# A gated delta-rule layer with a gated MLP: the first two groups' inverses made from two halves, and work moved between slots

## The chip, the core and the metric

The kernel runs on one core of a Trainium2 chip. Its engines are TensorE (PE in the profile), VectorE (DVE), ScalarE (ACT), GpSimd (POOL) and SyncE (SP), which here issues all DMAs. Each engine works through its own instructions in order and waits for others by semaphores. The metric is the device time of one execution in microseconds; the time before is 690.91 us, the median of 3 runs (690.77 to 692.4).

## The reference

```python
def _attn_ref(q, k, v, beta):                     # q, k, v: (4, 8, 768, 48)
    k_n = k / (np.linalg.norm(k, axis=-1, keepdims=True) + 1e-06)
    state = np.zeros((B, H, D, D))
    for t in range(S):
        kt, vt, bt = (k_n[:, :, t], v[:, :, t], beta[:, :, t, None])
        y[:, :, t] = np.einsum('bhd,bhde->bhe', q[:, :, t], state)
        v_old = np.einsum('bhde,bhd->bhe', state, kt)
        state = state + bt[:, :, :, None] * np.einsum('bhd,bhe->bhde', kt, vt - v_old)

def _moe_ref(x, w_gate, w_val, w_out):            # x: (3072, 384), d_ff = 1536
    gate = 1.0 / (1.0 + np.exp(-(x @ w_gate)))
    return (gate * (x @ w_val)) @ w_out
```

The first part is a recurrence over 768 tokens for 32 heads; its rows, put together over the heads, go through the gated MLP.

## The kernel before

**Groups.** The 768 tokens are cut into 12 groups of 64. A group is 64 tokens of all 32 heads (256 rows of x). Within a group the recurrence is solved in closed form: for each head the Gram matrix of its 64 keys is made (`gram`, L228), the norms of the keys are taken from its diagonal (`norms`, L182), and a triangular system of 32 rows is inverted on DVE for all heads at once (`solve`, L265): 31 columns from the last to the first, two DVE instructions each (L283, L286), over a tile X of 128 x 16 x 32, then a 32x32 block transposition into `mt` (L288). Two blocks of 32 tokens make up the 64: `updates` (L313) multiplies `mt` with the right-hand side of the first block (step 0), subtracts the coupling through L (step 1), and multiplies `mt` with the second block (step 2). The results U go from PSUM (`pu`) to SBUF (`su`) by four copies. `masked` (L247) makes the products of queries and keys (`pp`), which four DVE instructions mask (L260); `rows` (L339) makes the outputs from U, the masked products and the state; `advance` moves the state on; `flip` transposes the rows into x and splits them into a high and a low part for TensorE's float32r (`xx`).

**MLP.** For each group, 12 tiles f of 128 hidden units: `gate_val` (18 matmuls, `gv`), sigmoid on ACT, product on DVE (`gated`), a split into high and low parts (`split_hi` on ACT, `split_lo` on DVE, tile `h`), and `outp` (6 matmuls into `po`, which runs over all 12 tiles). `outp` runs LAG = 2 tiles behind `gate_val`.

**Weights.** They arrive as 36 pieces of 128 x 384 eight-byte words and are turned into two float32r parts by five instructions: two on ACT (`scaled`), a join on DVE (`u`), the high part on ACT (`weight_hi`), the low part on DVE (`weight_lo`). Before slot 0 the first 14 pieces are scaled; the other steps are spread over slots 0 to 20.

**Order.** The order of every engine's instructions is written out by hand. First comes a prologue for group 0 (L478 to L520). Then the program runs in slots: an MLP tile is two slots, `gate_val` at the start of the even one, `outp` at the start of the odd one; behind these come the functions that `plan[s]` lists, then the splits and the gating. Group g's attention runs in the slots of group g-1's MLP, which begin at slot w = 24(g-1). PSUM has four pools of two banks: `seq`, `aux`, `gv`, `po`. The two banks of `aux` hold in turn the Gram products, the masked products, `pu`, the rows and the flipped x, so each of these waits until the one before has been read.

Of the kernel before, what the change touches and what calls it, by code (L numbers as in the profile page):

```python
# [55 lines left out]
def deltanet_gated_mlp(ctx: ExitStack, tc: tile.TileContext, kd, qd, kv, beta, words, out):  # L56
# [20 lines left out]
    zero = const.tile([128, 1], F32, name="zero")  # L77
    xx = [const.tile([128, 2, KC, GT], F32R, name=f"xx{i}") for i in range(2)]

# [26 lines left out]
    def constants():  # L106
# [52 lines left out]
    def join(n):  # L159
        half, lo, hi = words_of(n)  # L160
        us[n] = u = wk.tile([128, PW], U32, name=f"u_{n}", tag="u", bufs=4)
        nc.vector.scalar_tensor_tensor(out=u, in0=hi, scalar=3, in1=lo, op0=ALU.logical_shift_left, op1=ALU.bitwise_or)  # L162
# [11 lines left out]
    def converting():  # L174
        for n in range(len(pieces) + 2):
            for m, fn in ((n, join), (n - 1, weight_hi), (n - 2, weight_lo)):
                if 0 <= m < len(pieces):
                    fn(m)
                yield

# [47 lines left out]
    def gram(g):  # L228
# [9 lines left out]
        for e in range(2):  # L238
            js = slice(e * J, (e + 1) * J)

            for lo, hi, o in ((0, 128, 0), (32, 64, 32), (96, 128, 32)):
                nc.scalar.copy(G[lo:hi, :, js], pg[e][lo:hi, :, o:o + 32].rearrange("q p t -> q t p"))  # L242
            for t in (0, 64):
                lo, o = t + 32 * e, 32 - 32 * e
                nc.scalar.copy(L[lo:lo + 32, js], pg[e][lo:lo + 32, :, o:o + 32])

# [18 lines left out]
    def solve(g):  # L265
# [47 lines left out]
    def updates(g, step):  # L313
# [5 lines left out]
        if step == 1:  # L319
# [6 lines left out]
            return  # L326
        pu = ps_aux.tile([128, J, D], F32, name=f"pu_{g}_{step}", tag="aux")
        for j in range(J):
            for e, x in KINDS:
                r = at[e, x][step // 2]  # L330
                nc.tensor.matmul(out=pu[r:r + 32, j], lhsT=mt[r:r + 32, e * J + j], rhs=R[e][r:r + 32, j], start=True, stop=True)  # L331
        for e, x in KINDS:
            r = at[e, x][step // 2]
            if g == 0 and x:
                nc.vector.tensor_copy(out=su[r:r + 32, 3 if x else e], in_=pu[r:r + 32])
            else:
                nc.scalar.copy(su[r:r + 32, 3 if x else e], pu[r:r + 32])  # L337

# [48 lines left out]
    def flip(g, c):  # L387

        st = state[g]
        if c == 0:  # L390
            st["xh"], st["xl"] = (xx[g % 2][:, i] for i in range(2))
# [25 lines left out]
    def split_hi(g, f):  # L417
        st = state[g]
        st["hh", f] = hh = wk.tile([128, 2, GT], F32R, name=f"h_{g}_{f}", tag="h", bufs=3)
        nc.scalar.copy(hh[:, 0], st["sg", f])  # L420
# [25 lines left out]
    W = 2 * NF  # L446
    LAG = 2
    plan = collections.defaultdict(list)
# [22 lines left out]

    NORMS, SOLVE = 18, 66
    conv = converting()


# [14 lines left out]
    stage(14, len(pieces))  # L490
    constants()
    gram(0)
# [16 lines left out]
    updates(0, 1)  # L509
    take(conv, 3)  # L510
    take(masks0, 2)
    updates(0, 2)
    take(masks0, 2)
    rows(0)
    take(conv, 3)
    load_k(2)
    load_q(2)
    flip(0, 0)
    flip(0, 1)
    take(conv, 3)  # L520
    ahead = 14
    pre1 = chain(norms(1), solve(1))
    spread(conv, 3 * (len(pieces) - 3), 0, W - 3)
    for n in range(ahead, len(pieces)):
        plan[(n - ahead) * 2 // 3].append(lambda n=n: scaled(n))
    spread(pre1, NORMS + SOLVE, 0, 12)
    plan[4].append(lambda: scale_v(1))
# [10 lines left out]
    for g in range(N):  # L538
# [89 lines left out]
```

## Time and profile before

| | |
|---|---|
| median of 3 runs | 690.91 us |
| profiled execution | 693.46 us, span 691.8 us, granted TensorE clock 0.967 |
| PE busy | 619.6 us (90%) |
| DVE busy | 490.7 us (71%) |
| ACT busy | 321.6 us (46%) |
| first gate_val of group 0 | 53.5 us |
| first gate_val of group 1 | 147.7 us |
| from one group to the next, later | 49.8 us |

How to read the rows: a row of the timeline is start, duration, engine, source line, operation, output tile <- input tiles, partitions x elements, and a count where equal instructions were merged; in brackets stands how long the engine had been idle and what ended that. "The chain of waits" is the chain of work that ended last, followed back from the end. The table of stretches gives, for each stretch of the span, the busy time of each engine, the granted clock of TensorE (1.00 is full speed), and DMA.

### The profile page before, as it was taken

To read this page: it belongs to the slowest core of one execution; us is meant where nothing else is said; L and a number is where in the kernel's file an instruction comes from. 1 tells how busy PE (TensorE), PEld (TensorE's weight loads), DVE (VectorE), ACT (ScalarE), POOL (GpSimd) and SP (SyncE) were. 2 spreads that over 40 slices of the span, in tenths; PEclk is the share of its full clock that TensorE was granted. 3 is DMA by queue.
4 is the path that set the end of the run, shared out by engine and by line. 5 is a ranking of instruction groups with operands and counts; after the bars stand their busy time and mean duration, and the time that the engine had idled before them with its cause. 6 is when DMAs were issued, how large, how long until landed. Compare 5 with 4: busy or idle time off the path is not lost.

```text
span 691.8 us, 22994 instructions
## 1 busy us (share of the span) xinstructions
PE 619.6 (90%) x9992; PEld 592.2 (86%) x9992; DVE 490.7 (71%) x1533; ACT 321.6 (46%) x877; POOL 7.4 (1%) x21
## 2 busy tenths in 40 slices
PE   3166755889999999999999999999999999999997
PEld 3155745889899999999999999999999999999996
DVE  4859498997796696687778778768768867852321
ACT  6827665734534634643543542543544445333322
POOL 4000000000000000000000000000000000000000
PEclk9999677989999999999999999999999999999999
DMA  9995000021021111211210211210210210010101
GB/s 262 338 400 123 21 5 1 2 78 47 4 79 47 24 57 48 57 42 31 79 25 26 79 25 26 79 36 15 79 48 3 79 26 3 1 25 4 24 1 23
DMA packets 17765, 41.00 MB, mean 59 GB/s; under 512 B 4224, under 2 KB 7296, under 8 KB 17664
## 3 DMA queue, kind: packets, MB, share of 16 engines
q1 hardware_dynamic: 17664, 39.53, 19.7%
q8 instruction: 78, 1.28, 0.8%
q14 instruction: 23, 0.19, 0.1%
HBM read 34.80 MB, written 4.72 MB: 57 GB/s over the span
## 4 chain that ended last, share of the span: by engine, by line
PE 70%; DVE 18%; DMA 5%; issue 3%; ACT 3%; SPq 1%; ACTq 0%; DVEq 0%
PE gv L409 37%; PE po L435 19%; DVE kqp L260 3%; PE pu L331 3%; DMA kv<-in_kv_dram 3%; DVE X L286 2%; DVE tmp L283 2%; DMA raw<-in_words_dram 2%; PE yy L360 2%; PE yy L357 2%; PE pg L237 2%; PE pk L300 2%; DVE gp L187 2%; DVE w L172 2%; DVE u L162 1%
## 5 line engine op out<-in xcount | busy, mean ns | idle before, releaser
L409 PE MATMUL gv<-xx,w 128*128 128x256 f32 x2592 | 350.9, 291 | 7.9 <-DVE w L172 5.5
L409 PEld LDWEIGHTS gv<-xx,w 128*128 128x128 f32 x2592 | 337.8, 197 | 12.3 <-DVE w L172 6.6
L435 PE MATMUL po<-w,h 128*128 128x384 f32 x864 | 183.6, 349 | 6.2 <-DVE h L425 6.2
L435 PEld LDWEIGHTS po<-w,h 128*128 128x128 f32 x864 | 146.5, 192 | 11.2 <-DVE h L425 7.9
L420 ACT CAST h<-sg 128x256 fp32r<-128x256 f32 x144 | 58.4, 405 | 178.4 <-DVE sg L415 178.0
L415 DVE TENSOR_TENSOR sg<-sg,gv 128x256 f32<-128x256 f32 x144 | 60.2, 418 | 71.9 <-ACT sg L414 70.8
L283 DVE TENSOR_TENSOR tmp<-X,gp 128x126 f32<-128x126 f32 (+22 forms) x372 | 94.6, 254 | 10.9
L286 DVE TENSOR_TENSOR X<-X,tmp 128x126 f32<-128x126 f32 (+22 forms) x372 | 94.7, 254 | 10.2
L425 DVE TENSOR_TENSOR h<-sg,h 128x256 fp32r<-128x256 f32 x144 | 60.5, 420 | 56.4 <-ACT h L420 56.1
L414 ACT ACTIVATE sg<-gv 128x256 f32<-128x256 f32 x144 | 55.2, 383 | 80.9 <-PE gv L409 80.1
L337 ACT COPY su<-pu 32x384 f32<-32x384 f32 x92 | 43.2, 470 | 23.0 <-PE pu L331 21.5
L226 ACT ACTIVATE kv<-kv,mq 128x48 f32<-128x48 f32 x192 | 44.5, 323 | 0.2 <-DVE mq L220 0.2
L242 ACT COPY G<-pg 32x256 f32<-32x256 f32 (+1 forms) x72 | 26.4, 367 | 20.0 <-PE pg L237 18.6
L237 PE MATMUL pg<-kqp 48*64 48x64 f32 x768 | 17.8, 245 | 19.7 <-DMA kqp<-in_kd_dram 10.0
L237 PEld LDWEIGHTS pg<-kqp 48*64 48x64 f32 x768 | 15.5, 156 | 22.7 <-issue 15.6
L260 DVE TENSOR_TENSOR kqp<-pp,pmask 64x512 f32<-64x512 f32 x48 | 32.9, 686 | 1.1
L331 PE MATMUL pu<-R,mt 32*32 32x48 f32 x1408 | 20.3, 206 | 11.5 <-DVE kqp L260 6.4
L331 PEld LDWEIGHTS pu<-R,mt 32*32 32x32 f32 x1408 | 17.4, 107 | 15.2 <-PE gv L409 6.6
L311 DVE TENSOR_TENSOR R<-kv,pk 128x384 f32<-128x384 f32 x44 | 22.3, 549 | 11.2 <-PE pk L300 9.9
L167 ACT CAST w<-u 128x384 fp32r<-128x384 f32 x36 | 18.2, 510 | 18.6 <-DVE u L162 18.4
L397 ACT CAST xx<-pt 128x384 fp32r<-128x384 f32 x24 | 11.5, 480 | 29.4 <-PE pt L395 29.3
L172 DVE TENSOR_TENSOR w<-u,w 128x384 fp32r<-128x384 f32 x36 | 19.7, 551 | 5.8 <-ACT w L167 5.7
(65 smaller groups left out, 417.5 us busy)
## 6 DMA issues: line engine op xcount, KB each, us to landing
raw<-in_words_dram SPq DMA_DIRECT2D x36, 384.0 KB, 7.8
kv<-in_kv_dram SPq DMA_DIRECT2D x24, 384.0 KB, 4.1
kqp<-in_qd_dram SPq DMA_DIRECT2D x24, 256.0 KB, 3.9
kqp<-in_kd_dram SPq DMA_DIRECT2D x24, 192.0 KB, 3.5
out_dram<-ot SPq DMA_DIRECT2D x48, 96.0 KB, 2.2
beta<-in_beta_dram SPq DMA_DIRECT2D x12, 16.0 KB, 3.8
```

What stands on the lines that cost most here:

```text
L226: nc.scalar.activation(V[:, c], V[:, c], AF.Copy, scale=mq[:, c, 0:1])
L237: nc.tensor.matmul(out=pg[e][t:t + 64, j], lhsT=kq[r:r + D, x, j], rhs=kq[r:r + D, x, j], start=True, stop=True)
L260: nc.vector.tensor_tensor(out=kq[t:t + 64, sec], in0=pp[e][t:t + 64], in1=pmask[t:t + 64, e].unsqueeze(1).to_broadcast([64, J, C]), op=ALU ...
L283: nc.vector.tensor_tensor(out=tmp, in0=X[:, k:16, j:j + 1].to_broadcast([128, n, j]), in1=gp[:, j:j + 1, 0:j].to_broadcast([128, n, j]), o ...
L286: nc.vector.tensor_tensor(out=X[:, k:16, 0:j], in0=X[:, k:16, 0:j], in1=tmp, op=ALU.add)
L331: nc.tensor.matmul(out=pu[r:r + 32, j], lhsT=mt[r:r + 32, e * J + j], rhs=R[e][r:r + 32, j], start=True, stop=True)
L409: nc.tensor.matmul(out=pg[:, o], lhsT=parts[w, f][:, a, k * 128:(k + 1) * 128], rhs=x[b][:, k], start=(k == 0 and q == 0), stop=(k == KC - ...
L414: nc.scalar.activation(h, st["gv", f][:, 0], AF.Sigmoid)
L415: nc.vector.tensor_tensor(out=h, in0=h, in1=st["gv", f][:, 1], op=ALU.mult)
L420: nc.scalar.copy(hh[:, 0], st["sg", f])
L425: nc.vector.tensor_tensor(out=hh[:, 1], in0=st["sg", f], in1=hh[:, 0].bitcast(F32), op=ALU.subtract)
L435: nc.tensor.matmul(out=po[s], lhsT=hh[:, a, ts], rhs=parts["o", f][:, w], start=(f == 0 and q == 0), stop=(f == NF - 1 and q == 2))
```

## The change

1. Groups 0 and 1 are solved by `solve_halves`: the two diagonal 16x16 blocks of each 32x32 system are inverted side by side (15 columns, two instructions each, on a tile of 128 x 2 x 8 x 16), put into X and transposed, and the lower left block is joined on TensorE by two sets of 64 matmuls of 32x32 (`pz`, `pm`), with a copy on ACT, a transposition and a subtraction on DVE. The lower left block is taken from G by `lower_left` (ACT, with a mask `under` as scale). Groups 2 to 11 keep `solve`.
2. In the prologue: G is copied ahead of L for both halves; group 1's Gram product comes behind group 0's solve instead of ahead of it; group 0's masks come ahead of and behind the first U; U of the two kinds goes through two PSUM banks, one copied by ACT and one by DVE; conversion has another order, and 8 pieces are scaled ahead instead of 14.
3. In the slots: the Gram product of group 2 moves from slot 3 to 14, its masked product from 6 to 22; the solve of group 2 starts in slot 16 instead of 13. For later groups the load moves from w-25 to w-30, the Gram product from w-21 to w-26, the masked product from w-18 to w-24 (group 3: w-27, w-24, w-22).
4. LAG is 3 instead of 2, with four `h` buffers instead of three and three `u` buffers instead of four; `xx` becomes a rotating tile that shares its place with the scratch of the join.

```diff
+    scratch = wk.tile([128, 3, CP, 32], F32, name="scratch", tag="xx", bufs=2)
...
+    def second_half(half):
+        nc.vector.tensor_reduce(out=under, in_=half, axis=AX.X, op=ALU.add)
...
     def converting():
+        todo = [(join, 0), (join, 1), (weight_hi, 0), (weight_hi, 1), (join, 2), (weight_lo, 0), (weight_lo, 1), (weight_hi, 2)]
+        for n in range(3, len(pieces) + 1):
+            todo += [(join, n), (weight_lo, n - 1), (weight_hi, n)] if n < len(pieces) else [(weight_lo, n - 1)]
...
                 nc.scalar.copy(G[lo:hi, :, js], pg[e][lo:hi, :, o:o + 32].rearrange("q p t -> q t p"))
+        for e in range(2):
             for t in (0, 64):
...
+    def lower_left(g):
+        a = scratch[:, 0]
+        nc.scalar.activation(a[:, :, 0:16].rearrange("q c t -> q t c"), state[g]["G"][:, 0:16], AF.Copy, scale=under)
...
+    def solve_halves(g):
+        for b in range(2):
+            nc.vector.tensor_tensor(out=H[:, b], in0=dmask[:, 8 * b:8 * b + 8, 16 * b:16 * b + 16], ...)
+            nc.vector.scalar_tensor_tensor(out=gs[:, b], in0=gp[:, 16 * b:16 * b + 16, 16 * b:16 * b + 16], scalar=-1.0, ...)
+        for j in range(15, 0, -1):
+            k, n = j // 2, 8 - j // 2
+            nc.vector.tensor_tensor(out=tmp, in0=H[:, :, k:8, j:j + 1]..., in1=gs[:, :, j:j + 1, 0:j]..., op=ALU.mult)
+            nc.vector.tensor_tensor(out=H[:, :, k:8, 0:j], in0=H[:, :, k:8, 0:j], in1=tmp, op=ALU.add)
+        nc.gpsimd.memset(X, 0.0)
+        for b in range(2):
+            nc.vector.tensor_copy(out=X[:, 8 * b:8 * b + 8, 16 * b:16 * b + 16], in_=H[:, b])
+        nc.vector.transpose(mt..., X...)
+        pool, tag = (ps_aux, "aux") if g else (ps_gv, "gv")
+        blocks(pz, A, mt)
+        nc.vector.transpose(D..., mt...)
+        nc.scalar.copy(Z, pz)
+        blocks(pm, D, Z)
+        nc.vector.tensor_tensor(out=mt, in0=mt, in1=pm, op=ALU.subtract)
...
-        pu = ps_aux.tile([128, J, D], F32, name=f"pu_{g}_{step}", tag="aux")
+        pu = [ps_aux.tile([128, J, D], F32, name=f"pu_{g}_{step}_{x}", tag="aux") for x in range(1 if g else 2)]
...
-    LAG = 2
+    LAG = 3
...
+    second_half(half)
+    lower_left(0)
     scaled(2)
-    scaled(3)
     scale_v(0)
+    for n in range(3, 8):
+        scaled(n)
+    for _ in solve_halves(0):
+        pass
     gram(1)
-    for n in range(4, 14):
-        scaled(n)
-    for _ in solve(0):
-        pass
+    lower_left(1)
+    take(masks0, 2)
     updates(0, 0)
-    take(conv, 6)
+    take(masks0, 2)
     updates(0, 1)
...
-    ahead = 14
-    pre1 = chain(norms(1), solve(1))
+    ahead = 8
+        plan[max(0, (n - ahead) * 2 // 3 - 1)].append(lambda n=n: scaled(n))
+    spread(chain(norms(1), solve_halves(1)), NORMS + HALVES, 0, 12)
...
-                plan[w - 25].append(lambda g=g: load_group(g))
-            plan[w - 21].append(lambda g=g: gram(g))
-            mask_later(g, w - 18)
-            spread(chain(norms(g), solve(g)), NORMS + SOLVE, w - 16 if g > 2 else w - 11, w + 9)
-            plan[w - 9 if g > 2 else w - 6].append(lambda g=g: scale_v(g))
+                plan[w - 30 if g > 3 else w - 27].append(lambda g=g: load_group(g))
+            plan[{2: 14, 3: w - 24}.get(g, w - 26)].append(lambda g=g: gram(g))
+            mask_later(g, {2: 22, 3: w - 22}.get(g, w - 24))
+            spread(chain(norms(g), solve(g)), NORMS + SOLVE, w - 16 if g > 2 else w - 8, w + 9)
+            plan[w - 9 if g > 2 else w - 3].append(lambda g=g: scale_v(g))
```

More of the change, by code (lines that the diff above doesn't have):

```diff
@@ L77, in deltanet_gated_mlp @@
     zero = const.tile([128, 1], F32, name="zero")
-    xx = [const.tile([128, 2, KC, GT], F32R, name=f"xx{i}") for i in range(2)]
+    under = const.tile([128, 1], F32, name="under")
+    scratch = wk.tile([128, 3, CP, 32], F32, name="scratch", tag="xx", bufs=2)
     state = [{} for _ in range(N)]
@@ L126, in constants @@
                 nc.gpsimd.affine_select(out=sl, in_=sl, pattern=[[1, C]], compare_op=ALU.is_gt, fill=0.0, base=-first, channel_multiplier=-1)
+        half = wk.tile([128, 4], F32, name="half", tag="half", bufs=1)
+        nc.gpsimd.memset(half, 1.0)
+        nc.gpsimd.affine_select(out=half, in_=half, pattern=[[-32, 4]], compare_op=ALU.is_ge, fill=0.0, base=-16, channel_multiplier=1)
+        nc.gpsimd.affine_select(out=half, in_=half, pattern=[[32, 4]], compare_op=ALU.is_ge, fill=0.0, base=31, channel_multiplier=-1)
+        nc.gpsimd.memset(scratch[:, 0], 0.0)
         make_identity(nc, ident)
+        return half
+    def second_half(half):
+        nc.vector.tensor_reduce(out=under, in_=half, axis=AX.X, op=ALU.add)
     pieces = [(0, "g"), (0, "v")]
@@ L160, in join @@
         half, lo, hi = words_of(n)
-        us[n] = u = wk.tile([128, PW], U32, name=f"u_{n}", tag="u", bufs=4)
+        us[n] = u = wk.tile([128, PW], U32, name=f"u_{n}", tag="u", bufs=3)
         nc.vector.scalar_tensor_tensor(out=u, in0=hi, scalar=3, in1=lo, op0=ALU.logical_shift_left, op1=ALU.bitwise_or)
@@ L174, in converting @@
     def converting():
[L175 to L179, printed above, removed]
+        todo = [(join, 0), (join, 1), (weight_hi, 0), (weight_hi, 1), (join, 2), (weight_lo, 0), (weight_lo, 1), (weight_hi, 2)]
+        for n in range(3, len(pieces) + 1):
+            todo += [(join, n), (weight_lo, n - 1), (weight_hi, n)] if n < len(pieces) else [(weight_lo, n - 1)]
+        for fn, n in todo:
+            fn(n)
+            yield
     def norms(g):
@@ L330, in updates @@
                 r = at[e, x][step // 2]
-                nc.tensor.matmul(out=pu[r:r + 32, j], lhsT=mt[r:r + 32, e * J + j], rhs=R[e][r:r + 32, j], start=True, stop=True)
+                nc.tensor.matmul(out=pu[0 if g else x][r:r + 32, j], lhsT=mt[r:r + 32, e * J + j], rhs=R[e][r:r + 32, j], start=True, stop=True)
         for e, x in KINDS:
@@ L334, in updates @@
             if g == 0 and x:
-                nc.vector.tensor_copy(out=su[r:r + 32, 3 if x else e], in_=pu[r:r + 32])
+                nc.vector.tensor_copy(out=su[r:r + 32, 3 if x else e], in_=pu[1][r:r + 32])
             else:
-                nc.scalar.copy(su[r:r + 32, 3 if x else e], pu[r:r + 32])
+                nc.scalar.copy(su[r:r + 32, 3 if x else e], pu[0][r:r + 32])
     def rows(g):
@@ L390, in flip @@
         if c == 0:
-            st["xh"], st["xl"] = (xx[g % 2][:, i] for i in range(2))
+            xx = wk.tile([128, 2, KC, GT], F32R, name=f"xx_{g}", tag="xx", bufs=2)
+            st["xh"], st["xl"] = (xx[:, i] for i in range(2))
         xh, xl, ys = st["xh"], st["xl"], st["ys"][:, c].rearrange("p h e d -> p (h e d)")
@@ L418, in split_hi @@
         st = state[g]
-        st["hh", f] = hh = wk.tile([128, 2, GT], F32R, name=f"h_{g}_{f}", tag="h", bufs=3)
+        st["hh", f] = hh = wk.tile([128, 2, GT], F32R, name=f"h_{g}_{f}", tag="h", bufs=4)
         nc.scalar.copy(hh[:, 0], st["sg", f])
@@ L470, in take @@
             next(gen, None)
-    NORMS, SOLVE = 18, 66
+    NORMS, SOLVE, HALVES = 18, 66, 40
     conv = converting()
@@ L490, in deltanet_gated_mlp @@
     stage(14, len(pieces))
-    constants()
+    half = constants()
     gram(0)
```

43 lines of the change are left out of this document (34 added, 9 removed).

## The prediction

> **What bounds the kernel now.** I read the slices of the span first, then the chain that ended last, then busy times by stage, then the timeline of the first 150 us.
>
> ```profile
> span 691.8 us, 22994 instructions
> ...
> PE   3166755889999999999999999999999999999997
> ...
> DVE  4859498997796696687778778768768867852321
> ```
> ```profile
> 54.13 3.99 PE gv L409 x17
> ...
> 148.92 4.00 PE gv L409 x17
> ...
> 221.80 1.14 DVE gp L187
> ...
> 271.59 1.13 DVE gp L187
> ```
> ```profile
> 54.00:149.00 95.00, 66.67 (x956) 59.68 (x955) 80.27 (x229) 60.51 (x157) 0.00 (x0) 0.80 0.14 36
> 222.00:272.00 50.00, 49.34 (x842) 47.61 (x842) 38.10 (x123) 22.64 (x64) 0.00 (x0) 1.00 0.16 44
> ```
>
> The last fence gives, after the length of a stretch, busy PE, weight loads, DVE, ACT and POOL, then the granted clock. There are three stages. Until 54.1 us a serial chain makes group 0's rows; from there to 148.9 us group 0's MLP tiles run beside weight conversion and group 1's solve; from 148.9 us on TensorE is the bound. In the second stage DVE is busy 80.3 of 95 us, and TensorE runs at 0.80 of its clock: DVE sets the pace, ACT follows at 60.5. In steady state a group takes 49.8 us (271.59 - 221.80) and TensorE idles 0.66 of 50. So a microsecond taken from the first two stages is worth a microsecond, and in the third only a TensorE wait counts.
>
> **The change, part by part: the first chain.**
>
> ```profile
> 8.04 0.73 ACT L245 COPY L<-pg 32x256 f32<-32x256 f32 x2
> 9.97 1.25 DVE L187 STREAM_TRANSPOSE gp<-G 128x1024 f32<-128x1024 f32 x1 [4.20 <-ACT G L242]
> ...
> 15.13 0.68 DVE L274 TENSOR_TENSOR X<-dmask,gam 128x512 f32<-128x512 bf16 x1
> 15.73 1.02 DVE L272 SCALAR_TENSOR_TENSOR gp<-gp,gam 128x512 f32<-128x512 f32 x2
> 16.67 0.18 DVE L283 TENSOR_TENSOR tmp<-X,gp 128x31 f32<-128x31 f32 x1
> ...
> 17.56 0.22 DVE L283 TENSOR_TENSOR tmp<-X,gp 128x58 f32<-128x58 f32 x1
> 17.82 0.22 DVE L286 TENSOR_TENSOR X<-X,tmp 128x58 f32<-128x58 f32 x1
> ...
> 18.59 2.54 PE L237 MATMUL pg<-kqp 48*64 48x64 f32 x64 [5.66 <-DMA kqp<-in_kd_dram]
> ...
> 34.63 0.71 DVE L288 STREAM_TRANSPOSE mt<-X 128x512 f32<-128x512 f32 x1
> 35.60 1.50 PE L331 MATMUL pu<-kv,mt 32*32 32x48 f32 x64 [14.47 <-DVE mt L288]
> 37.22 0.96 ACT L337 COPY su<-pu 32x384 f32<-32x384 f32 x2 [3.41 <-PE pu L331]
> 38.27 1.14 DVE L335 COPY su<-pu 32x384 f32<-32x384 f32 x2 [2.92 <-ACT su L337]
> ```
>
> The old solve lasts from 15.13 to 35.34, 20.2 us. The new one: two dmask products of 128 elements and two scalings of 256 (0.27 and 0.37 each, between the small rows and L272) 1.3 us; 30 steps of 16 to 72 elements, started 0.21 to 0.27 us apart as the old steps of those sizes were (58 elements: 17.56 to 17.82), 7.35; two copies 0.4; the transposition 0.7: 9.8 us. The join has no row. Its 64 matmuls of 32x32 are nearest to the 64 of pu, 1.50 us here (at the other end half of that), twice; Z's copy out of PSUM, a third more than one L337 with 128 partitions, 0.6; the subtraction 0.7; four hand-overs 0.8: 5.1 us, bounded by 3.5 and 7; D's transposition hides under pz. G copied ahead of L saves 0.7 (L245 at 8.04), the reduction for the mask costs 0.2. So mt stands at 35.3 - 20.2 + 9.8 + 5.1 - 0.5 = 29.5.
>
> [...]
>
> Then group 1's Gram product, moved behind the solve, stands ahead of U on TensorE (2.54 us, row 18.59), and on ACT its ten copies, 3.8 us (a G triple of 1.15 and an L pair of 0.74, each twice: rows 259.31 and 262.38 below), and the 0.4 us of lower_left stand ahead of the two U copies. ACT ends them at about 36.3, where DVE ended its pair at 39.4: 3.1 left. In the third step the copies from two banks run side by side, which saves 1.1 (38.27 waited for ACT).
>
> ```profile
> 45.63 1.41 DVE L260 TENSOR_TENSOR kqp<-pp,pmask 64x512 f32<-64x512 f32 x2
> ...
> 47.09 1.74 PE L357 MATMUL yy<-su,kqp 64*64 64x48 f32 x54 [0.28 <-DVE kqp L260]
> ```
>
> The masks that held the rows until 47.09 now run under U: 1.2 more. Gate_val of group 0 starts at 54.1 - 5.4 = 48.7, with 4 to 6.5 as bounds of the gain.
>
> **Slots 0 to 12** (a slot is half an MLP tile).
>
> ```profile
> 72.18 0.44 PE L237 MATMUL pg<-kqp 48*64 48x64 f32 x2 [9.26 <-issue]
> ...
> 79.60 0.56 DVE L172 TENSOR_TENSOR w<-u,w 128x384 fp32r<-128x384 f32 x1 [5.73 <-ACT w L167]
> ...
> 81.67 3.71 ACT L226 ACTIVATE kv<-kv,mq 128x48 f32<-128x48 f32 x16
> ...
> 85.82 0.42 DVE L415 TENSOR_TENSOR sg<-sg,gv 128x256 f32<-128x256 f32 x1 [3.49 <-ACT sg L414]
> ...
> 106.47 0.55 DVE L162 SCALAR_TENSOR_TENSOR u<-raw 128x384 uint32<-128x384 uint32 x1
> 106.94 0.56 DVE L172 TENSOR_TENSOR w<-u,w 128x384 fp32r<-128x384 f32 x1
> ...
> 115.98 0.71 DVE L288 STREAM_TRANSPOSE mt<-X 128x512 f32<-128x512 f32 x1
> ```
>
> DVE ends slot 11 at 116.6 now. There go: 20.2 - 10.5 us of the solve on DVE; group 2's four masks, 2.8 (4 of 0.7, as at 45.63); and DVE's wait of 5.7 behind group 2's Gram copies. There come: a round trip to TensorE and ACT in slot 11, in which nothing else is queued on DVE, 3.6 us with the late sigmoid behind it; about 2 more conversion instructions (0.47 apart, 106.47 to 106.94), 1.0; more waits on ACT, which scales two pieces more, 1.5. The 3.5 behind scale_v stays. Sum: 9.7 + 2.8 + 5.7 - 3.6 - 1.0 - 1.5 = 12.1 gained, and slot 12 starts at 116.6 - 5.4 - 12.1 = 99.1.
>
> **Slots 12 to 24.**
>
> ```profile
> 88.77 0.54 ACT L153 ACTIVATE raw<-raw 128x384 int32<-128x384 uint16 x1
> 89.21 0.53 ACT L155 ACTIVATE raw<-raw 128x384 f32<-128x384 f32 x1
> ```
>
> Part of it is given back. ACT has eight pieces to scale here instead of four (0.88 a piece, two instructions 0.44 apart): 3.5. Group 2's Gram product now comes in slot 14, behind the U copies of slot 13 whose PSUM buffer it needs; its 3.8 us of copies stand ahead of the sigmoid that DVE waits for, and DVE has no solve step left to fill with: 3.8. Group 2's product for the masks (1.1) now stands between the last flip and group 1's first tile, and a late end of scale_v, 1.0. Sum 9.4. Gate_val of group 1 starts at 148.9 - 5.4 - 12.1 + 9.4 = 140.8.
>
> **Steady state and end.**
>
> ```profile
> PE pu L331 <- DVE kqp L260: 6.4, 9, 1.2
> ```
> ```profile
> 252.16 0.41 DVE L415 TENSOR_TENSOR sg<-sg,gv 128x256 f32<-128x256 f32 x1
> ...
> 255.00 0.41 DVE L415 TENSOR_TENSOR sg<-sg,gv 128x256 f32<-128x256 f32 x1
> ...
> 259.19 2.42 PE L409 MATMUL gv<-xx,w 128*128 128x256 f32 x18
> ...
> 259.31 1.15 ACT L242 COPY G<-pg 128x256 f32<-128x256 f32 x3 [0.42 <-PE pg L237]
> ...
> 261.45 1.21 PE L435 MATMUL po<-w,h 128*128 128x384 f32 x6
> ...
> 262.38 0.74 ACT L245 COPY L<-pg 32x256 f32<-32x256 f32 x2
> ...
> 262.49 2.32 PE L409 MATMUL gv<-xx,w 128*128 128x256 f32 x18
> ```
>
> Nine times U waits for a PSUM buffer that the next group's masks hold, 6.4 us in all; with the masks six slots earlier this goes. But the product for the masks (pp) now comes two slots after the Gram product, not three, and needs its two buffers. ACT has emptied them 3.93 us after the Gram matmuls (259.19 to 263.12). TensorE arrives after one po and one gv, 3.3 us (259.19 to 262.49 is such a pair). So pp waits 0.63, nine times: 5.7. The same copies hold the sigmoid back, and masks follow at once on DVE, so that gate_val's PSUM bank may come late by 0 to 0.6; I take 0.2, nine times 1.8. Group 2's solve has 44 steps and four masks left behind slot 24: 0 to 3.3, I take 0.5. Output a tile further behind moves one po (1.05) from the stage where TensorE waits to the one where it doesn't. Sum: 1.05 - 6.4 + 5.7 + 1.8 + 0.5 = 2.7 lost. Earlier loads wait on SP for kqp and kv only, off the path; the end (copy and store) is as it was.
>
> Net 8.1 - 2.7 = 5.4 us. The profiled execution has 693.5 us around its span of 691.8; the median of the runs shown is 690.9. Taking 5.4 from the median, and 0.5 for conversion in an order that has pieces ready sooner, gives 685.
>
> **Rivals.**
> - *ACT keeps up* in slots 12 to 24. Its work in 54 to 149 rises from 60.5 to about 68 us, below the 80 left there; against it speaks that copies come in lumps. Without the 7.3 of scaling and Gram copies: 678.
> - *No wait at pp* nor behind it, for instance because TensorE arrives later than I think: 7.5 less, 677.5.
> - *The array warms.* The 64 pu matmuls took 1.50 us in the chain, although the granted clock stands at 1.00 there, and joins leave fewer idle gaps ahead of the later ones. Were pu, pk, pu at 0.9 and yy at two thirds, the chain would end 3 us sooner: 682. [...]
> - *Nothing is left*: DVE's backlog at slot 34 costs the 3.3 and each group the full 0.6: 685 + 2.8 + 3.6 = 691.
> - *Slower.* In steady state DVE is 3.9 us late behind the Gram copies and gets its masks (2.8) at once, with little slack: its work for a tile is 2.84 us (sg at 252.16 to sg at 255.00), TensorE's 3.3 (259.19 to 262.49). From 1.5 us of new waits per group on (0.63 at pp, the rest for gate_val's bank), the 8.1 of the start are eaten. At 2.0 per group: 9 x (2.0 - 0.83) = 10.5 more, 695.5.
>
> **How the numbers follow.** Forecast 0.38, ACT keeps up 0.16, no wait at pp 0.10, warm array 0.05, nothing left 0.13, slower 0.18. A change under 0.3% (2.1 us) can't be told from none here. The three faster rivals and most of the forecast's case (0.33 of 0.38) make faster 0.64; nothing left and the rest of the forecast's case 0.16; slower 0.20. The likeliest case alone reaches from 681 to 690. The range, 673 to 696, takes in both unknowns of the join, two gains together, and the slower case up to its price.
>
> **What would show it.** A first gv near 48.7 shows the chain; the mt subtraction of group 1 ending near 99 shows slots 0 to 12; a DVE wait for the sigmoid of 3 us or more right behind group 2's Gram copies, and group 1's first gv near 141, show what is given back. In the waits, pu behind kqp must be gone, and pp behind ACT's L copies must stand with about 0.6 nine times. A pitch of 49.2 us between groups, or one above 50.5, would prove me wrong, and so would a first tile of group 1 before 134 us.

## The result and the profile after

The changed kernel takes 711.52 us (median of 4 runs, 709.65 to 712.71). The kernel before, run beside it, takes 690.84 us. The ratio is 1.029, with a 95% interval of 1.027 to 1.032. The prediction said 685 us with a range from 673 to 696; the sign was wrong. The profiled execution took 712.71 us with a span of 711.0.

The head of the page, as for the kernel before:

```profile
span 711.0 us, 23982 instructions
...
PE   3248748779899999999999999999999999999997
```

Only the first eleven slices (to 196 us) differ from the row of before, and behind them TensorE is as full as it was. A slice is 17.8 us, so the digits show neither a stall of a few us nor a longer pitch (the time from one group to the next); for these the rows are read.

TensorE by rows in the first chain (start, duration, engine, line and operation; in brackets its idle time and what ended that):

```profile
24.43 1.93 PE L345 MATMUL pz<-mt,scratch 32*32 32x32 f32 x128 [11.71 <-DVE mt L338]
27.05 0.65 PE L345 MATMUL pm<-scratch 32*32 32x32 f32 x30 [0.69 <-ACT scratch L349]
32.20 1.54 PE L345 MATMUL pm<-scratch 32*32 32x32 f32 x98 [4.50 <-issue]
33.67 1.12 PE L250 MATMUL pg<-kqp 48*64 48x64 f32 x29
38.37 1.33 PE L250 MATMUL pg<-kqp 48*64 48x64 f32 x35 [3.59 <-issue]
42.75 0.37 PE L396 MATMUL pu<-kv,mt 32*32 32x48 f32 x4 [3.05 <-ACT L L259]
43.51 1.49 PE L396 MATMUL pu<-kv,mt 32*32 32x48 f32 x60 [0.39 <-ACT L L259]
45.45 1.50 PE L388 MATMUL pk<-su,L 32*32 32x48 f32 x28 [0.44 <-ACT su L402]
48.88 1.01 PE L388 MATMUL pk<-su,L 32*32 32x48 f32 x36 [1.93 <-issue]
50.58 1.96 PE L396 MATMUL pu<-kv,mt 32*32 32x48 f32 x64 [0.69 <-DVE kv L376]
53.57 1.27 PE L422 MATMUL yy<-su,kqp 48*64 48x48 f32 x27 [1.03 <-ACT su L402]
56.28 1.31 PE L422 MATMUL yy<-su,kqp 64*64 64x48 f32 x37 [1.44 <-issue]
...
62.30 2.03 PE L475 MATMUL gv<-xx,w 128*128 128x256 f32 x6 [0.57 <-ACT xx L463]
```

Two things stand here that the prediction didn't have. First, four stalls (4.50, 3.59, 1.93, 1.44 us) are put down to "issue": nothing that the profile shows was awaited. From one to the next there are 98 + 29 = 127, 35 + 64 + 28 = 127, and 36 + 64 + 27 = 127 matmul records (each of these f32 matmuls shows as two). With their weight loads that is about 254 instructions, at even distances. Second, U waits 3.05 us for ACT's copies of group 1's Gram tiles.

In the same stretch the DMA engines are full of weights. The first fence is the table of stretches (length, busy PE, weight loads, DVE, ACT, POOL, granted clock, DMA share, GB/s), the second the list of DMA queues:

```profile
30.00:35.00 5.00, 2.59 (x127) 2.34 (x127) 1.19 (x2) 0.00 (x0) 0.00 (x0) 1.00 1.02 389
...
40.00:50.00 10.00, 4.24 (x128) 3.18 (x128) 2.51 (x5) 4.95 (x13) 0.00 (x0) 1.00 1.03 397
```
```profile
q8 instruction: 82, 1.34, 0.8%
```

The instruction queue moves 82 packets and 1.34 MB, so 16.3 KB each. TensorE has 10504 matmul records and as many weight loads, which is 256 instructions for each of these packets, so they are taken for TensorE's.

The start of each packet is in the trace. In the first chain they start at 29.82, 35.87, 46.45 and 53.48 us and take 1.1 to 1.5 us, and TensorE goes on 1.27 to 1.44 us after each has landed: these are the ends of the four stalls. Each packet starts only after TensorE has entered the block before it: at 24.84 us, counted 127 records back from the first stall, then at 32.20, 38.37 and 48.88. That it is this entering that sends for the packet is inferred from the order. By it, the 11.71 us for which TensorE sat idle ahead of `pz` couldn't help: the block that `pm` lacked from 27.70 us on was sent for 0.4 us into `pz`. In the kernel before, TensorE enters blocks at 19.96, 39.95, 47.58 and 59.07 us, so at least 7.6 us apart, beside the same weights, and no row of its first chain has such a stall.

**Where the 19.2 us of span went** (691.8 to 711.0):

| stretch | before | after | difference |
|---|---|---|---|
| start to first gv of group 0 | 53.54 | 62.30 | +8.8 |
| from there to first gv of group 1 | 94.19 | 97.15 | +3.0 |
| from there to group 3's gp (the transposition that begins its norms and solve), and on to group 4's | 24.23 + 49.76 | 26.59 + 49.00 | +1.6 |
| seven pitches, group 4's gp to group 11's | 348.5 (49.78 each) | 353.4 (50.49 each) | +4.9 |
| from there to the end | 121.6 | 122.6 | +1.0 |

The pitch comes from the two ends of this row of seven:

```profile
235.04 1.20 DVE L200 STREAM_TRANSPOSE gp<-G 128x1024 f32<-128x1024 f32 x1
...
588.44 1.20 DVE L200 STREAM_TRANSPOSE gp<-G 128x1024 f32<-128x1024 f32 x1
```

### The profile page after: what moved, and what is told of

It reads as the page before. It is cut to its first block, busy times and chain, and to the rows that moved or that the text cites. A ratio compares the mean times of both kernels' runs of the same rounds, so it can differ in the third digit from the quotient of the medians.

```text
span 711.0 us, 23982 instructions
## 1 busy us (share of the span) xinstructions
PE 634.8 (89%) x10504; PEld 601.9 (85%) x10504; DVE 474.7 (67%) x1480; ACT 320.1 (45%) x881; POOL 9.3 (1%) x27
## 3 DMA queue, kind: packets, MB, share of 16 engines
q8 instruction: 82, 1.34, 0.8%
## 4 chain that ended last, share of the span: by engine, by line
PE 64%; DVE 19%; ACT 10%; issue 4%; DMA 1%; SPq 1%; ACTq 0%; DVEq 0%
PE gv L475 33%; PE po L501 16%; DVE kqp L274 4%; ACT G L255 3%; DVE tmp L297 3%; DVE X L300 3%; PE pu L396 3%; ACT L L259 2%; DVE sg L481 2%; PE pg L250 2%; PE yy L422 2%; PE yy L425 2%; PE pk L365 1%; DVE h L491 1%; PE pk L388 1%
## 5 line engine op out<-in xcount | busy, mean ns | idle before, releaser
L475 PEld LDWEIGHTS gv<-xx,w 128*128 128x128 f32 x2592 | 334.1, 195 | 19.2 <-DVE sg L481 7.2
L501 PE MATMUL po<-w,h 128*128 128x384 f32 x864 | 185.9, 352 | 0.0
L486 ACT CAST h<-sg 128x256 fp32r<-128x256 f32 x144 | 58.4, 405 | 203.9 <-DVE sg L481 203.9
L297 DVE TENSOR_TENSOR tmp<-X,gp 128x126 f32<-128x126 f32 (+22 forms) x310 | 78.8, 254 | 8.8
L300 DVE TENSOR_TENSOR X<-X,tmp 128x126 f32<-128x126 f32 (+22 forms) x310 | 78.9, 254 | 8.4
L480 ACT ACTIVATE sg<-gv 128x256 f32<-128x256 f32 x144 | 55.1, 383 | 53.6 <-PE gv L475 52.7
L402 ACT COPY su<-pu 32x384 f32<-32x384 f32 x92 | 43.3, 470 | 25.6 <-PE pu L396 24.3
L269 PE MATMUL pp<-kqp 48*64 48x64 f32 x768 | 19.9, 243 | 8.8 <-DVE xx L464 4.8
L269 PEld LDWEIGHTS pp<-kqp 48*64 48x64 f32 x768 | 16.6, 154 | 12.2 <-DVE xx L464 5.2
L463 ACT CAST xx<-pt 128x384 fp32r<-128x384 f32 x24 | 11.5, 479 | 28.0 <-PE pt L461 27.9
```

The costliest lines, as they stand in the source:

```text
L297: nc.vector.tensor_tensor(out=tmp, in0=X[:, k:16, j:j + 1].to_broadcast([128, n, j]), in1=gp[:, j:j + 1, 0:j].to_broadcast([128, n, j]), o ...
L300: nc.vector.tensor_tensor(out=X[:, k:16, 0:j], in0=X[:, k:16, 0:j], in1=tmp, op=ALU.add)
L475: nc.tensor.matmul(out=pg[:, o], lhsT=parts[w, f][:, a, k * 128:(k + 1) * 128], rhs=x[b][:, k], start=(k == 0 and q == 0), stop=(k == KC - ...
L480: nc.scalar.activation(h, st["gv", f][:, 0], AF.Sigmoid)
L501: nc.tensor.matmul(out=po[s], lhsT=hh[:, a, ts], rhs=parts["o", f][:, w], start=(f == 0 and q == 0), stop=(f == NF - 1 and q == 2))
```

## The experiments

All are timed against the kernel before on the same chip. "First gv" is group 0's, and the pitch is the mean of seven, as above. "Clear chain" stands for the early Gram product together with the weights from the 10th piece later. Where an edit has several places, the diffs show the last or the one that is new, with `...` for the others.

| kernel | median us | ratio to before, interval | first gv | pitch |
|---|---|---|---|---|
| weights from the 15th piece later | 706.47 | 1.021 (1.019 to 1.023) | 56.3 | 50.48 |
| group 0 by the old solve | 699.95 | 1.012 (1.010 to 1.013) | 50.0 | 50.49 |
| old places, LAG 3 | 719.81 | 1.040 (1.038 to 1.043) | 62.8 | 51.46 |
| kernel before, with dummy matmuls | 692.70 | 1.002 (1.001 to 1.003) | 55.3 | 49.8 |
| LAG 2 | 710.95 | 1.028 (1.026 to 1.030) | 61.7 | 50.49 |
| LAG 2, old places | 702.39 | 1.016 (1.014 to 1.018) | 62.2 | 49.86 |
| the same, group 0 by the old solve | 691.53 | 0.999 (0.998 to 1.000) | 49.5 | 49.85 |
| the same, group 2 at its old places | 693.20 | 1.001 (0.999 to 1.003) | 50.2 | 49.86 |
| early Gram product | 702.02 | 1.015 (1.013 to 1.017) | 52.7 | 50.48 |
| early Gram product, weights from the 10th piece later | 697.09 | 1.008 (1.007 to 1.010) | 46.6 | 50.48 |
| group 0 by the old solve, LAG 2, masked product later | 695.65 | 1.006 (1.004 to 1.007) | 49.9 | 50.03 |
| clear chain, LAG 2, masked product later | 692.88 | 1.002 (1.001 to 1.004) | 47.3 | 50.04 |
| clear chain, LAG 2, old places | 688.20 | 0.996 (0.994 to 0.997) | 46.4 | 49.85 |
| clear chain, LAG 2, Gram product in an odd slot | 685.48 | 0.992 (0.990 to 0.993) | 47.2 | 49.48 |

### The first chain: weights, instruction blocks and a Gram product

**Weights later.**

```diff
-    stage(14, len(pieces))
     ...
     load_q(2)
+    stage(14, len(pieces))
```

> The changed kernel with one edit: the loads of weight pieces 14 to 35 stand behind group 2's k and q on SP, so that they start when group 0's rows are done (about 50 us) and not at 25 us. Theory A (TensorE's instructions come in blocks over the same DMA engines, and behind the weights each block takes 6 us and more): the four stalls put down to issue in the prologue (4.5, 3.6, 1.9, 1.4 us) fall below 1 us each, the first gate_val comes at 50 to 53 us instead of 62.9, and the time falls by 8 to 12 us to about 700. Rival B (the stalls are waits that the trace does not name, or lie in TensorE itself): first gate_val at 61 or later, time within 2 us of 711.5. Rival C (the weights are then late for conversion): first gate_val at 50 to 53, but the first tile of group 1 no earlier than 156, time 706 or more.

First gv came 6.0 us earlier, at 56.3, and the time fell by 5.0 us: the right way, but less than theory A had (50 to 53 us and about 700). TensorE in this kernel:

```profile
32.63 1.54 PE L345 MATMUL pm<-scratch 32*32 32x32 f32 x98 [4.99 <-issue]
...
36.34 1.33 PE L250 MATMUL pg<-kqp 48*64 48x64 f32 x35 [1.11 <-issue]
```

The DMA share fell from 1.02 to 0.17 between 30 and 40 us. The first stall stayed, because pieces 10 to 14 and group 1's loads were still on their way (a DMA share of 1.06 between 20 and 30 us); the second shrank to 1.11; the third and fourth are gone. The conversion didn't lack the weights: from first gv of group 0 to group 1's it took 97.3 us, as in the changed kernel.

**Group 0 by the old solve**, everything else changed.

```diff
-    for _ in solve_halves(0):
+    for _ in solve(0):
```

> The changed kernel with the old solve for group 0 alone (256 matmul records and as many weight loads fewer on TensorE in the prologue; group 1 keeps the halves). Theory A: two blocks of instructions fewer, so the stalls shrink; mt comes at about 34 instead of 34.5 us, the first gate_val at 55 to 58 us, and the time falls by 4 to 8 us. Rival D (the new order, with group 1's Gram product and its copies ahead of U, is what makes the chain late, and the join costs little): first gate_val at 61 to 64, time within 2 us of 711.5.

First gv stands at 50.0, 12.3 us earlier than with the halves and earlier than either theory had. The join's 256 records ahead of U are gone, group 1's Gram product finds TensorE idle and runs near 18 us, and U no longer waits for ACT. So the faster inverse made the chain slower. The time is still 8 us above the kernel before although first gv is 3.5 earlier: more than 11 us are lost behind it.

**Dummy matmuls in the kernel before**, 256 records put where TensorE is idle.

```diff
     gram(1)
+    for rep in range(2):
+        dm = ps_gv.tile([128, CP, 32], F32, name=f"dummy_{rep}", tag="gv")
+        ... # the 64 matmuls of 32x32 of one set of the join, on ident
```

> The kernel before with 128 added matmuls of 32x32 (256 records and 256 weight loads, 512 instructions), whose product nobody reads, behind group 1's Gram product, where TensorE is idle for 14 us waiting for mt. Theory A: mt still comes at 35.3 us and the dummies take only idle time, but two more blocks must be fetched behind the weights, so stalls put down to issue appear behind mt and the first gate_val comes at 58 to 66 us instead of 54.1; the time rises by 4 to 12 us. Rival B: the dummies are hidden, first gate_val within 1 us of 54.1, time within 1.5 us of 690.8.

```profile
20.38 1.50 PE L507 MATMUL dummy<-ident 32*32 32x32 f32 x94
24.80 1.93 PE L507 MATMUL dummy<-ident 32*32 32x32 f32 x128 [2.92 <-issue]
32.64 0.69 PE L507 MATMUL dummy<-ident 32*32 32x32 f32 x34 [5.91 <-issue]
...
41.70 1.01 PE L323 MATMUL pk<-su,L 32*32 32x48 f32 x35 [1.48 <-issue]
```

Matmuls that wait for nothing stall every 128 records too, 2.92 and 5.91 us, in a kernel that has nothing of the change. These two fell into time in which TensorE was idle anyway. The third, 1.48 us in `pk`, lies on the path: in the kernel before, the same `pk` runs through from 39.46 us without a stall. First gv came 1.8 us later, nearly all of it the price of this one stall; the median rose by 0.6 us, where theory A had 4 to 12. The boundaries cost nothing in the first chain of the kernel before, which enters its blocks 7.6 us or more apart, and 11.5 us in that of the changed one: there 128 records of 32x32 run in 1.93 us (`pz`), and beside the weights a block takes 6.2 to 10.5 us from the moment at which the block before it is entered to TensorE's going on.

**Early Gram product**, then with the **weights from the 10th piece later** too.

```diff
+    gram(1)
     for _ in solve_halves(0):
         pass
-    gram(1)
     lower_left(1)
...
```

> The changed kernel with group 1's Gram product ahead of group 0's solve, as in the kernel before; weights untouched. Theory A (TensorE loses time in the first chain where it reaches a new block of its instructions while the weights fill the DMA, and U waits for ACT to copy group 1's Gram tiles): the product runs in TensorE's idle time near 18 us, U's wait of 3.05 us for ACT's L copies goes, and so do 2.4 us of Gram matmuls from the chain and one block of 128 records; the stall of 4.5 in pm stays, one of about 3.6 comes in U instead of the Gram product. First gv at 55 to 57, time 704 to 706. Rival (the copies on ACT only collide elsewhere): first gv above 60.

> As the run with the early Gram product, and all weight pieces from the tenth on are queued behind group 2's keys and queries, so that only 9 of 36 pieces are on their way while the chain runs. Theory A: no stall is left, mt is joined at 29.5 to 30 and first gv of group 0 comes at 48 to 49.5, which is what the prediction had (48.7); time 711.5 - 13.5 = 697 to 699, or up to 3 more if the weights are then late for conversion. Rival (a new block costs TensorE 4 to 5 us after an idle stretch whatever the DMA does): the stall in pm stays, first gv at 52 to 54.

With the Gram product alone first gv came at 52.7, earlier than either theory had, and 9.5 us of the 20.7 were back: U's wait, the Gram matmuls and part of the stalls (3.78, 1.37 and 0.31 are left). With the weights later as well:

```profile
24.21 1.50 PE L345 MATMUL pz<-mt,scratch 32*32 32x32 f32 x94 [3.69 <-DVE mt L338]
26.15 0.74 PE L345 MATMUL pz<-mt,scratch 32*32 32x32 f32 x34 [0.44 <-issue]
28.40 1.49 PE L345 MATMUL pm<-scratch 32*32 32x32 f32 x93 [1.52 <-ACT scratch L349]
30.25 0.74 PE L345 MATMUL pm<-scratch 32*32 32x32 f32 x35 [0.36 <-issue]
31.77 1.50 PE L396 MATMUL pu<-kv,mt 32*32 32x48 f32 x64 [0.78 <-DVE mt L353]
...
46.61 4.59 PE L475 MATMUL gv<-xx,w 128*128 128x256 f32 x18 [0.57 <-ACT xx L463]
```
```profile
25.00:30.00 5.00, 2.94 (x180) 2.54 (x169) 0.00 (x0) 3.82 (x10) 0.00 (x0) 1.00 0.37 80
30.00:35.00 5.00, 3.28 (x129) 2.71 (x132) 3.63 (x6) 0.94 (x2) 0.00 (x0) 1.00 0.02 3
```

The first boundary that stalls in this chain costs 0.44 and the next 0.36 us, where the changed kernel had 4.50 and 3.59. The two are short for different reasons. For the first, the early Gram product had TensorE enter the block before at 19.35 us, so its packet came at 23.62, still beside full DMA engines (a share of 1.05 between 20 and 25 us). For the second, the packet started at 27.38, 1.23 us after the block before was entered, and the stretch has 80 GB/s. The rival, a fixed price of a new block after an idle stretch, falls. First gv at 46.6 is 1.4 us better than the lower end of what was expected, and 6.9 better than before the change. What a packet waits for between the entering of the block before and its start (5.0 us ahead of the changed kernel's first stall) isn't shown; that it takes less with the weights out of the way is.

### Later groups: places and LAG

**Old places, LAG 3.**

```diff
-                plan[w - 30 if g > 3 else w - 27].append(lambda g=g: load_group(g))
-            plan[{2: 14, 3: w - 24}.get(g, w - 26)].append(lambda g=g: gram(g))
-            mask_later(g, {2: 22, 3: w - 22}.get(g, w - 24))
+                plan[w - 25].append(lambda g=g: load_group(g))
+            plan[{2: 14}.get(g, w - 21)].append(lambda g=g: gram(g))
+            mask_later(g, {2: 22}.get(g, w - 18))
```

> The changed kernel with the old places of load, Gram product and masked product for groups 3 to 11 (w-25, w-21, w-18). If the moved places make the steady state slower: the pitch between groups falls from 50.49 to 49.8 us, the waits of pp for ACT's L copies go, those of U for masks come back (0.66 a group), and the time falls by 5 to 7 us. If it is the lag of three tiles or the buffers: pitch 50.3 or more, time within 2 us of 711.5.

This fell altogether: 719.81 us, slower than the changed kernel. In the waits between 215 and 600 us (engine and tile waiting, what for: us in all, times, longest) stand two that no other kernel has in this size:

```profile
PE pu L396 <- DVE kqp L274: 15.5, 8, 3.0
...
DVE R L376 <- DMA out_dram<-ot: 9.8, 8, 2.3
```

R shares three buffers with `ot`, the copy of the output that the store reads. With LAG 3 that store comes in slot 5 of the next group, one slot ahead of R; DVE waits for it, is late with its masks, and U waits for these, 1.9 us a group. So LAG 3 with the old places has a cost of its own, and this run says nothing of what the new places cost.

**LAG 2 with the new places, and LAG 2 with the old.**

```diff
-    LAG = 3
+    LAG = 2
```

> The changed kernel with its output two tiles behind gate_val again (LAG 2) and nothing else; the Gram and masked products of later groups stay at their new places. Theory P (the lost 0.69 us per group comes from the new places: pp waits for ACT's copies, and pk and pp are no longer neighbours): pitch between groups stays at 50.4 to 50.5, pp still waits 0.5 to 0.6 for ACT's L copies, and only the shorter tail, about 1 us, is gained: 710 to 711. Theory Q (the later output is the cause: tiles that share a place with it, or the buffers of h): pitch 49.8 to 49.9 and 704 to 706. If LAG 2 brings a new wait with the new places, the pitch rises above 50.6 and the time above 713.

> The changed kernel with LAG 2 and, from group 3 on, load, Gram product and masked product at the old places. Theory P and theory Q both say that the steady state is the old one again: pitch 49.8, U waits again for the masks (6 us in nine), R no longer waits for the store of the output, and the time is 711.5 - 6.2 - 1 = 704 to 705. If the pitch stays at 50.3 or more, something else of the change (four h buffers, three u buffers, the rotating xx) costs the time, and both theories fall.

With the new places the pitch stays at 50.49, with the old ones it is 49.86. So at LAG 2 the new places cost the 0.63, and LAG costs nothing of it (theory P). LAG alone gave back 0.6 us of the median. The second kernel is 2 us better than either theory had, because the stretch with the end of group 2's solve and group 3's products is shorter too: from group 2's gp to group 3's and on to group 4's it takes 46.9 + 51.4 us instead of 52.0 + 49.0. One group's stretch in the two shows of what the 0.63 is made. LAG 2 with new places:

```profile
264.97 2.32 PE L475 MATMUL gv<-xx,w 128*128 128x256 f32 x18
267.23 0.33 PE L269 MATMUL pp<-kqp 48*64 48x64 f32 x2
267.81 1.16 PE L269 MATMUL pp<-kqp 48*64 48x64 f32 x62 [0.26 <-ACT L L259]
268.89 1.31 PE L501 MATMUL po<-w,h 128*128 128x384 f32 x6
...
275.42 1.58 PE L501 MATMUL po<-w,h 128*128 128x384 f32 x6
276.84 2.41 PE L475 MATMUL gv<-xx,w 128*128 128x256 f32 x18
```

LAG 2 with old places:

```profile
275.08 1.15 PE L365 MATMUL pk<-su,kqp 48*64 48x48 f32 x64
276.05 1.14 PE L269 MATMUL pp<-kqp 48*64 48x64 f32 x64
277.12 1.32 PE L501 MATMUL po<-w,h 128*128 128x384 f32 x6
...
281.49 2.32 PE L475 MATMUL gv<-xx,w 128*128 128x256 f32 x18
284.45 0.88 PE L396 MATMUL pu<-R,mt 32*32 32x48 f32 x64 [0.64 <-DVE kqp L274]
```

From pp's start to po's it is 1.66 us in the first and 1.07 in the second: +0.59 for the wait. One po is late (start to next start 1.42, usually 1.06): +0.36; with LAG 3 it is a gv by the same 0.36. pp no longer follows pk directly; from the start of a gv to the next start it takes 2.26 us where another shape follows, against 2.16, from that of pk 1.08 against 0.97, and from that of a po that follows another shape 1.15 against 1.06: +0.3. So in these rows a change of tile shape costs about 0.1 us on each end of it. On the other side U starts 2.96 us after gate_val in the second, 2.25 in the first: -0.71. The sum, +0.54, is near the 0.63.

**Masked product two slots later** (with the old solve for group 0 and LAG 2), and the same with the clear chain.

```diff
...
-            mask_later(g, {2: 22, 3: w - 22}.get(g, w - 24))
+            mask_later(g, {2: 22, 3: w - 20}.get(g, w - 22))
```

> The changed kernel with group 0 solved as before, LAG 2, and the later groups' masked product two slots after its new place (w-22, group 3: w-20), so four slots behind their Gram product. Theory S (the pitch of 50.48 is made of pp's wait for ACT's copies, 0.6, of a gate_val or output matmul that comes 0.36 late behind the lump of copies and masks on ACT and DVE, and of 0.3 for three more switches of TensorE's tile shape, less the 0.7 of U's wait that is gone): pp doesn't wait, the late 0.36 goes, the 0.3 stays, U doesn't wait for masks: pitch 49.4 to 49.5, time 687 to 689, faster than the kernel before. Rival T (the masks only push DVE's lateness to another place): pitch 49.8 to 50.4, 691 to 697.

> The run with the clear chain (both groups by halves, early Gram product, weights behind) with LAG 2 and the masked product at w-22. If theories A and S hold together: 698 - 1 - 9 x 1.05 = 687 to 689, the same as with the old inverse for group 0 or 1 to 2 us better. If S falls: 691 to 696. If A falls: 692 or more.

pp's wait is gone, but the pitch is 50.03, not 49.4, and theory S falls: a gate_val still waits for DVE's product, although the masks now come later.

```profile
257.26 2.41 PE L475 MATMUL gv<-xx,w 128*128 128x256 f32 x18 [0.30 <-DVE sg L481]
```

So the masks weren't what made it late. The second kernel came to 692.88 rather than 687 to 689 for the same reason. A reading of ACT's rows in the kernel with LAG 2 gave the next theory: the Gram product stands in an even slot there, and its copies stand ahead of the sigmoid (L480) of the tile that has just been made.

```profile
263.93 2.31 ACT L255 COPY G<-pg 128x256 f32<-128x256 f32 x6 [1.71 <-PE pg L250]
266.26 1.50 ACT L259 COPY L<-pg 32x256 f32<-32x256 f32 x4
267.78 0.38 ACT L480 ACTIVATE sg<-gv 128x256 f32<-128x256 f32 x1
```

**Clear chain with LAG 2 and the old places, and with the Gram product in an odd slot.**

```diff
...
-                plan[w - 30 if g > 3 else w - 27].append(lambda g=g: load_group(g))
-            plan[{2: 14, 3: w - 24}.get(g, w - 26)].append(lambda g=g: gram(g))
-            mask_later(g, {2: 22, 3: w - 22}.get(g, w - 24))
+                plan[w - 30 if g > 3 else w - 25].append(lambda g=g: load_group(g))
+            plan[{2: 14, 3: w - 21}.get(g, w - 25)].append(lambda g=g: gram(g))
+            mask_later(g, {2: 22, 3: w - 18}.get(g, w - 22))
```

> The changed kernel with the clear chain (early Gram product, weights from the tenth piece on behind group 2's keys and queries), LAG 2, and the later groups' loads, Gram products and masked products at the old places; both groups still solved by halves. If the causes named so far are all and add up: 697.1 (clear chain alone) - 9.1 (what LAG 2 and old places took from the changed kernel, 711.5 to 702.4) = 688, pitch 49.8, 0.4 to 0.5 % faster than the kernel before. If the early start of group 0 is given back in the weight conversion once the later stages are short again: 690 to 691.5, the time of the run with the old inverse for group 0.

> As the run beside it, but from group 4 on the Gram product at w-25 (an odd slot, one slot behind the change's place) and the masked product three slots behind it, at w-22. Theory V (in an even slot the Gram copies stand on ACT ahead of the sigmoid of the tile just made, and gate_val or the output comes 0.4 late; in an odd slot they stand ahead of the split into parts only): no gate_val waits for DVE's product, pp doesn't wait, U doesn't wait for the masks; the price is 0.4 for two more switches of shape. Pitch 49.85 - 0.72 + 0.42 = 49.55, time 2 to 3 below the run beside it. Rival W (the wait comes from the masks following at once on DVE): gate_val or U still waits 0.4 or more, pitch 49.9 to 50.1, time 0 to 2 above the run beside it.

The first came to 688.20, the 688 of the sum: the causes named so far add up. Its first gv is 7.2 us earlier than in the kernel before and its time only 2.8 us shorter; 2.3 of the difference is lost in slots 0 to 24, below. The second has a pitch of 49.48, where theory V had 49.55, and 685.48 us, 0.8% below the kernel before. In an odd slot the copies stand ahead of the split (L486) only, and no gate_val, pp or U waits in this kernel's steady state:

```profile
247.08 2.32 ACT L255 COPY G<-pg 128x256 f32<-128x256 f32 x6 [1.72 <-PE pg L250]
249.41 1.50 ACT L259 COPY L<-pg 32x256 f32<-32x256 f32 x4
250.94 0.41 ACT L486 CAST h<-sg 128x256 fp32r<-128x256 f32 x1
251.37 0.38 ACT L480 ACTIVATE sg<-gv 128x256 f32<-128x256 f32 x1
```

Against the kernel beside it, which differs from group 4 on only, that is 2.7 us: 0.37 for each pitch. The test of theory V is the clear chain with the masked product two slots later: from group 4 on it has the Gram product one slot earlier, in the even slot, and nothing else different, and its pitch is 50.04. So this slot is worth 0.56 us a group.

### Slots 0 to 24

LAG 2 and the old places with **group 0 by the old solve**, then with **group 2 at its old places** as well.

```diff
...
-            plan[{2: 14}.get(g, w - 21)].append(lambda g=g: gram(g))
-            mask_later(g, {2: 22}.get(g, w - 18))
-            spread(chain(norms(g), solve(g)), NORMS + SOLVE, w - 16 if g > 2 else w - 8, w + 9)
-            plan[w - 9 if g > 2 else w - 3].append(lambda g=g: scale_v(g))
+            plan[w - 21].append(lambda g=g: gram(g))
+            mask_later(g, w - 18)
+            spread(chain(norms(g), solve(g)), NORMS + SOLVE, w - 16 if g > 2 else w - 11, w + 9)
+            plan[w - 9 if g > 2 else w - 6].append(lambda g=g: scale_v(g))
```

> As the run with LAG 2 and the old places, and group 0 solved as before; what is left of the change is group 1's inverse by halves, the new prologue order and group 2's new places. If the parts add up: 700.0 (old inverse for group 0) - 7 (steady state) = 692 to 694, so no better than before within 0.3 %: group 1's halves bring nothing. First gv of group 0 at 50, of group 1 at 146 to 147. If the steady state isn't mended by the old places: 699 to 700.

> The run before this one with group 2 at its old places too (Gram product in slot 3, masked product in slot 6, solve from slot 13): what is left is group 1's inverse by halves and the new prologue order. Theory D (DVE and ACT have a fixed amount of work in slots 0 to 24, and group 2's work is only moved inside them): first gv of group 1 within 1.5 us of that run's, time within 0.3 % of it. Theory E (the lumps cost: group 2's Gram copies in slot 14 and its masked product behind the last flip stall DVE and TensorE, while in slot 3 they lie beside conversion): first gv of group 1 at 141 to 144 and 687 to 690, faster than the kernel before. Against: the round trip of the halves in slot 11 may find the buffers of aux taken by group 2's products, then first gv of group 1 at 149 or later.

With only group 1's halves, the new prologue order, the changed buffers and group 2's places left, the time is 691.53, no different from before. Group 2's places don't matter to it either (theory D): first gv of group 1 comes 96.8 us after group 0's with the new places and 95.6 with the old, and 94.2 in the kernel before, which solves group 1 in full. So group 1's halves, together with the new order of conversion, gain nothing there, though they take work off DVE. The table of stretches and the waits of the changed kernel show why:

```profile
62.90:159.60 96.70, 69.80 (x1204) 62.98 (x1205) 72.29 (x203) 66.41 (x172) 0.00 (x0) 0.79 0.10 28
```
```profile
DVE sg L481 <- ACT sg L480: 10.6, 4, 4.7
DVE w L183 <- ACT w L178: 6.3, 7, 3.4
DVE mt L353 <- PE pm L345: 4.8, 1, 4.8
```

DVE is busy for 72.3 us instead of 80.3, but waits 21.7 us instead of the 11.1 before (5.7 and 5.4). The 8.0 us saved turned into 10.6 us of waiting. Of these, 5.8 are for ACT, which does 66.4 us of work here instead of 60.5, and 4.8 for the join's own matmuls. Six pieces that were scaled in the prologue are scaled here now, 5.3 us of ACT's work at 0.88 a piece. No run put them back, so what the halves alone would have done in this stretch stays open.

That group 2's work was only moved shows in the two halves of the stretch, which part where group 1's inverse is done (100.96 and 109.98 us). With the new places slots 0 to 12 take 51.5 us and slots 12 to 24 45.3; with the old ones 59.8 and 35.8. So group 2's two products cost about 9.5 us behind slot 12 and 8.3 ahead of it (with the old places its solve also starts three slots sooner).

## Why the prediction was wrong, step by step

- **The inverse on DVE** was right: 9.8 us predicted, 14.47 to 24.3 measured, and the transposed halves reached TensorE at 24.43.
- **The join** was sized right at 5.1: without the 4.50 stall it took 5.5 (24.43 to 34.47). That pz and pm were priced by 64 records of pu was a slip: 64 matmuls are 128 records here, 1.93 us each instead of 1.50.
- **"mt stands at 29.5" and first gv at 48.7: the step that failed.** The join was costed by durations alone. What it does besides, it puts 256 records into TensorE's stream in front of U while weights fill the DMA, and the stream stalls 11.5 us in all. In the step "group 1's Gram product ... stands ahead of U" the 2.54 us were counted, and the copies only as being ahead of U's copies; that U over both banks must wait until ACT has emptied the Gram tiles (3.05) was overlooked. The two make 14.5 us. By the row that the table uses (53.54 before, where the prediction counted from 54.1) the prediction's first gv is 48.1, so it was missed by 14.2. With the Gram product early and the weights later, so without nearly all of both, first gv came at 46.6.
- **Slots 0 to 12**: 12.1 us of gain predicted, 11.4 measured (63.1 from first gv to slot 12 before, 51.7 after: mt's subtraction ends at 114.0). Right.
- **Slots 12 to 24**: 9.4 predicted to be given back, 14.3 measured. The terms that were mis-sized are group 2's two products: 3.8 + 1.1 were counted, and the runs with and without them there differ by 9.5. One part is seen: the product for the masks, costed at 1.1, waits 3.63 and 1.16 us for the flipped x to be read out of the two banks, and then takes 1.98 us. The two stretches together lose 3.0 where 2.7 were to be gained.
- **Group 2's solve behind slot 24**: 0.5 taken out of 0 to 3.3. The changed kernel loses 2.4 up to group 3's gp and wins 0.8 back by the next.
- **Steady state.** U's waits went (-0.71 a group, as said) and pp's wait came (0.59, as said: 0.63). The lateness was taken at 0.2 and measured 0.36, within its bounds; 0.3 for three more switches of tile shape wasn't in the sum. Its cause was named half right: the copies ahead of the sigmoid are it, the masks are not.
- **LAG**: 1.05 predicted; 1.0 at the end of the trace, 0.6 in the median.
- **The warm array** didn't come: with the chain cleared the 64 records of pu took 1.50 us, as before the change. At the other end of the kernel before 64 records of the same shape take 0.88 (at 628.07 us), which is 0.59 of that, where the prediction had half; the granted clock is 1.00 in both places, and no run shows what makes the difference.
- **The slower rival** had the sign by the wrong mechanism: new waits of 2.0 a group, where the pitch rose by 0.7 and the larger part of the loss lay in the first 160 us.

The loss was put on the wrong side by the chain: there an estimate off by 14.2 us (48.1 to 62.3) outweighs all other errors, 5.7 in slots 0 to 24 and 4.8 behind them.

## What to carry to other kernels

In the changed kernel's first chain instructions cost more than their duration: TensorE's stream stalled 11.5 us in all at the bounds of its instruction blocks, beside a DMA share of 0.75 to 1.04. So in a stage in which the DMA engines are full, look for idle times put down to "issue" at even distances, compare them with the packets of the instruction queue, and count how many instructions an edit puts on the path there and how fast they run through a block. A part that is moved takes its readers along: before a product is put in front of another, see which engine empties its PSUM bank and what stands behind that engine's copies. And work taken from the busiest engine is only a gain if the engines that feed it have time to spare in the same stretch; here 8.0 us of work on DVE became 10.6 us of waiting, for ACT and for the new part's own matmuls.

## What was not expected of the hardware

- Stalls of TensorE every 127 to 128 matmul records (some 256 instructions with their weight loads), 0.3 to 5.9 us long. In the first chain each ends 1.3 to 1.6 us after a 16 KB packet of the instruction queue has landed, and the packet starts only after the block before has been entered; 11.7 us of idle time ahead of that moment brought nothing. From the entering to TensorE's going on it took 6.2 to 10.5 us in stretches with a DMA share of 0.75 to 1.04, and 3.7 us in one with 0.03 (weights later, 32.63 to 36.34; 0.17 over 30 to 40 us).
- A change between matmul shapes in steady state cost about 0.1 us on either side at a granted clock of 1.00, so the order that keeps equal shapes together (pk and pp) was worth 0.3 us a group here.
